# Sharing filler matmuls evenly over attention steps in a fused attention and gated-FFN block on one core

## The chip, the core and the metric

One core of a Trainium2 chip runs the whole program. The core has a matmul engine (TensorE, PE in the profile, with its weight loads shown as PEld), VectorE (DVE), ScalarE (ACT), GpSimd (POOL), and SyncE (SP), which here only issues transfers. Each engine works through its own list of instructions in order; they meet through semaphores. Matmuls write into PSUM, eight banks of 128 x 512 float32 numbers; DVE and ACT move results from there to SBUF.

The metric is the time of one execution on the device in microseconds (us). The kernel before is given by three runs, of which the median counts.

## The reference

A transformer block in which attention and a gated feed-forward part run side by side on the same normalized input. S = 2048 tokens, D = 448, H = 16 heads of 28, window W = 256, F = 1792, all bfloat16:

```python
xn = layernorm(x)                                   # over D, eps 1e-5, no weights
q, k, v = split(xn @ wqkv)                          # 16 heads of 28
scores = q @ k.T * 28 ** -0.5
mask = (0 <= i - j) & (i - j < 256)                 # causal, sliding window
o = softmax(where(mask, scores, -1e9)) @ v
out = x + o @ wo + (gelu(xn @ w_gate) * (xn @ w_up)) @ w_down
```

## The kernel before

The tokens are worked in four blocks of 512 (QB, index `qb`), each of four tiles of 128. A block has these kinds of work:

- **prep** (`stat`, `rstd`, `norm`, driven by the generator `gen_prep`): mean and variance on DVE, the reciprocal root on ACT, the normalized rows on DVE; nine small operations a block, handed out one at a time as `aux`.
- **proj** (`gen_proj`): four transposes of normalized tiles on PE, copied to `xnT` by DVE; four head groups of q and k (`pq`, `pk`, cast to `qT` and `kT`); four tiles of v in pairs (`pv`, cast to `v_sb`). The contraction of 448 is three chunks of 128 and one of 64; `mm3` makes the three, `mm_half` the last, two at a time on the two halves of the array.
- **attention** (`attention`): twelve steps, for each of four head groups three pieces `n` of keys. A step makes QK (`sc`, eight small matmuls, four heads side by side), two exponentials on ACT to `p_sb`, and masks on POOL. PV (`ov`, in `finish`) of a step is issued two steps later (`lag`). After the third piece of a group DVE normalizes: transpose of ov (line 328), copy of the sums (329), reciprocal (331), transpose back (333), product to `oN` (334).
- **gates** (`gated`): seven pairs of the 14 chunks of F: gate (`gt`) and up (`u0`) matmuls, gelu on ACT, product on DVE into `hT`. The up part of chunks listed in `early` has been made ahead, by `gen_up`, into `hT`.
- **down** (`gen_down`): for each token tile 18 matmuls into `po` (four of `wo` with oN, 14 of `wd` with hT), the residual added by DVE, and the output transfer issued by SP.

The source order is the order of every engine's list (`tc.manual_schedule()`). Attention alone doesn't fill PE, so generators of other matmuls are interleaved with it as filler, through the class `Feed`: each `yield` names nanoseconds, and `feed.run(ns)` advances the first generator until that much is spent. In a step before, `feed.run(per_step * 0.6)` stands after the masks and `feed.run(per_step * 0.4)` after the PV. What a call spends over its budget is not carried on.

In block 0 proj(0) is made ahead of attention, and the filler is proj(1) and the early up part of four pairs. In blocks 1 and 2 the filler is down of the block before and proj of the next one. In block 3 it is down(2) and the up part of all seven pairs. After the steps the last two PVs are issued, then `feed.drain()` runs what is left, then come the gates.

PSUM before: tag `s`, two tiles of two banks each, for `sc` and `gt`; tag `m`, four banks, for all else, ov included. A tile of a tag waits until the last reader of the tile whose bank it takes has finished.

At the end, a check of all softmax sums (`okc`, `nok`, `flag`) decides whether `general_path`, a slow exact version, has to run; with these inputs it does not. `n_ok` is loaded into a register of every engine after the last tile of down.

## Time and profile before

| | us |
|---|---|
| median of three runs | 290.64 |
| lowest and highest of the three | 289.18, 291.83 |
| profiled execution, device time | 290.42 |
| profiled execution, span from first to last instruction | 288.7 |

The mean granted clock of TensorE in the profiled execution is 0.925 of full speed. The profile lists instructions by engine, source line and tile name, with starts in us from the beginning of the span. Time of an engine inside a stage is read from a table of stretches: each row has the stretch, its length, and then the busy time of PE, PEld, DVE, ACT and POOL, each with the number of instructions, the granted clock, the share of DMA and its GB/s. Other rows are from the list in order of time (start, duration, engine, line, operation, tile written and tiles read, count, and in brackets the idle time before it with what ended it) and from the chain of work that ended last (start, duration, engine, tile, line).

### The profile page before, as it was taken

The page shows a single profiled execution, that of the slowest core. Times are in us where ns is not written, and L with a number is a line of the kernel's source. Part 1 is how long each engine was busy: PE and PEld are TensorE (multiplying, and loading weights), DVE is VectorE, ACT ScalarE, POOL GpSimd, SP SyncE. Part 2 cuts the span into 40 slices and gives each one's busy share as a digit, 9 for nine tenths or more (in the row PEclk, how much of TensorE's full clock was granted, in tenths as well). Part 3 has the DMA queues.
Part 4 walks back from the last instruction along what each step waited for, and adds up shares of the span by engine and source line. Part 5 has one row for each costly group of instructions (what it writes and reads, how often), then busy time and mean ns, then how long its engine had stood idle before and what let it go on. Part 6 is the DMA issues. An engine that isn't in the chain of part 4 may idle for free.

```text
span 288.7 us, 4252 instructions
## 1 busy us (share of the span) xinstructions
PE 253.2 (88%) x1704; PEld 96.9 (34%) x1725; DVE 154.7 (54%) x296; ACT 135.3 (47%) x156; POOL 75.8 (26%) x104
## 2 busy tenths in 40 slices
PE   8997989599999994799999896699999999479992
PEld 3433322223344331233344332233334322123451
DVE  6587887953432979533321677353431396643510
ACT  3535435833654458423365348713364525756300
POOL 6203323600053435300042334600014233530000
PEclk9999979779999997599999999589999999759998
DMA  6999300000010000000000000000001100000011
GB/s 199 372 263 283 102 2 0 1 2 0 0 33 17 16 3 0 3 0 0 0 18 32 18 0 2 0 0 2 0 0 34 33 0 2 0 0 2 0 34 40
DMA packets 9025, 10.94 MB, mean 38 GB/s; under 512 B 616, under 2 KB 7976, under 8 KB 9000
## 3 DMA queue, kind: packets, MB, share of 16 engines
q1 hardware_dynamic: 8312, 9.69, 11.3%
q10 hardware_dynamic: 688, 0.92, 1.0%
q8 instruction: 15, 0.25, 0.4%
q14 instruction: 10, 0.08, 0.1%
HBM read 8.77 MB, written 1.84 MB: 37 GB/s over the span
## 4 chain that ended last, share of the span: by engine, by line
PE 75%; ACT 11%; DVE 7%; issue 3%; POOL 2%; ACTq 0%; POOLq 0%
PE po L233 15%; PE gt L177 14%; ACT p_sb L349 10%; PE u L177 7%; PE sc L344 5%; PE ue L177 5%; PE gt L182 5%; PE po L229 4%; PE pv L177 4%; PE pk L177 3%; PE pq L177 3%; PE ov L323 3%; PE wps L134 3%; POOL p_sb L355 2%; PE pq L182 2%
## 5 line engine op out<-in xcount | busy, mean ns | idle before, releaser
L349 ACT ACTIVATE p_sb<-sc 128x1024 bf16<-128x1024 f32 (+2 forms) x96 | 87.8, 968 | 66.7 <-PE sc L344 66.6
L355 POOL TENSOR_SCALAR_AFFINE_SELECT p_sb<-p_sb 128x512 bf16<-128x512 bf16 (+1 forms) x92 | 69.8, 781 | 175.9 <-ACT p_sb L349 175.9
L233 PE MATMUL po<-wd,hT 128*128 128x448 bf16 x224 | 48.3, 353 | 0.0
L177 PE MATMUL gt<-xnT,wg 128*128 128x512 bf16 x161 | 46.0, 399 | 1.4 <-issue 1.4
L295 DVE TENSOR_TENSOR hT<-ge,u 128x512 bf16<-128x512 bf16 x34 | 21.8, 684 | 34.2 <-ACT ge L293 34.2
L344 PE MATMUL sc<-qT,kT 32*128 32x128 bf16 (+2 forms) x352 | 24.7, 291 | 15.2 <-ACT p_sb L349 13.8
L293 ACT ACTIVATE ge<-gt 128x1024 bf16<-128x1024 f32 x17 | 17.4, 1024 | 41.9 <-PE gt L177 41.9
L238 DVE TENSOR_TENSOR res<-po,x_sb 128x448 bf16<-128x448 f32 x16 | 10.0, 624 | 44.9 <-PE po L233 44.9
L177 PE MATMUL u<-xnT,wu 128*128 128x512 bf16 x99 | 28.8, 394 | 0.2
L323 PE MATMUL ov<-p_sb,v_sb 128*32 128x128 bf16 (+2 forms) x352 | 22.6, 323 | 6.0 <-POOL p_sb L355 5.8
L233 PEld LDWEIGHTS <-hT 128*128 128x128 bf16 x224 | 20.4, 98 | 20.8 <-issue 3.8
L177 PEld LDWEIGHTS <-wg 128*128 128x128 bf16 x168 | 14.3, 101 | 24.8 <-issue 13.4
L177 PEld LDWEIGHTS <-wu 128*128 128x128 bf16 x168 | 15.3, 101 | 21.0 <-issue 7.2
L344 PEld LDWEIGHTS <-kT 32*128 32x128 bf16 x352 | 8.1, 93 | 33.5 <-issue 33.2
L328 DVE STREAM_TRANSPOSE l<-ov 128x512 f32<-128x512 f32 x16 | 11.4, 710 | 14.9 <-PE ov L323 14.9
L177 PE MATMUL ue<-xnT,wu 128*128 128x512 bf16 x62 | 18.4, 406 | 0.4 <-issue 0.3
L281 ACT ACTIVATE ge<-gt 128x1024 bf16<-128x1024 f32 x11 | 11.3, 1024 | 13.6 <-PE gt L177 13.6
L182 PE MATMUL gt<-xnT,wgu 64*128 64x512 bf16 x45 | 15.1, 398 | 0.0
L229 PE MATMUL po<-wo,oN 128*128 128x448 bf16 x64 | 14.8, 353 | 0.0
L323 PEld LDWEIGHTS <-v_sb 128*32 128x32 bf16 x352 | 7.0, 99 | 22.7 <-issue 19.8
L177 PE MATMUL pq<-xnT,wqp 128*128 128x512 bf16 x45 | 12.9, 381 | 1.8 <-DVE xnT L173 1.6
L282 DVE TENSOR_TENSOR hT<-ge,hT 128x1024 bf16<-128x1024 bf16 x11 | 7.6, 693 | 12.3 <-ACT ge L281 12.3
(67 smaller groups left out, 247.8 us busy)
## 6 DMA issues: line engine op xcount, KB each, us to landing
out_dram<-res SPq DMA_DIRECT2D x16, 112.0 KB, 1.7
wd<-in_B_w_down_dram SPq DMA_DIRECT2D x1, 1568.0 KB, 13.3
wu<-in_B_w_up_dram SPq DMA_DIRECT2D x1, 1344.0 KB
wg<-in_B_w_gate_dram SPq DMA_DIRECT2D x1, 1344.0 KB, 16.3
x_sb<-in_A_x_dram SPq DMA_DIRECT2D x1, 896.0 KB
wraw<-in_A_wqkv_dram ACTq DMA_DIRECT2D x1, 672.0 KB
x_sb<-in_A_x_dram SPq DMA_DIRECT2D x1, 448.0 KB
wo<-in_A_wo_dram SPq DMA_DIRECT2D x4, 98.0 KB
```

The lines of the kernel that those rows point to most:

```text
L177: nc.tensor.matmul(ps, lhsT=lhs(c), rhs=rhs(c), start=start and c == 0, stop=stop and c == 2, skip_group_check=True)
L182: nc.tensor.matmul(ps, lhsT=lhs[p0:p0 + 64], rhs=rhs[p0:p0 + 64], start=start, stop=stop, tile_position=(p0, 0), skip_group_check=True)
L229: nc.tensor.matmul(po[:, 0:D], lhsT=oN[:, g, cs], rhs=wo[:, g, :], start=(g == 0), stop=False, skip_group_check=True)
L233: nc.tensor.matmul(po[:, 0:D], lhsT=hT[:, f, cs], rhs=wd[:, f, :], start=False, stop=(f == NF - 1), skip_group_check=True)
L281: nc.scalar.activation(out=ge[:, :, :], in_=gt[:, :, :], func=ACT.Gelu_apprx_tanh)
L293: nc.scalar.activation(out=ge[:, :, :], in_=gt[:, :, :], func=ACT.Gelu_apprx_tanh)
L295: nc.vector.tensor_tensor(out=hT[:, f + i, :], in0=ge[:, i, :], in1=us[i][:, :], op=ALU.mult)
L323: nc.tensor.matmul(ov[32 * j:32 * j + 32, q0:q0 + nq], lhsT=v_sb[:, kt, h, :], rhs=p_sb[:, j, col:col + nq], start=(n == 0 and i == 0), st ...
L328: nc.vector.transpose(out=l1[:, :, :].rearrange("p a b -> p (a b)"), in_=ov[:, :])
L344: nc.tensor.matmul(ss[j // 2][:, j % 2, col:col + nq], lhsT=kT[r, g, kt * P:(kt + 1) * P], rhs=qT[r, g, qb * QB + q0:qb * QB + q0 + nq], s ...
L349: nc.scalar.activation(out=p_sb[:, 2 * i:2 * i + 2, 0:ncol], in_=ss[i][:, :, 0:ncol], func=ACT.Exp, scale=SCALE)
L355: nc.gpsimd.affine_select(out=reg, in_=reg, pattern=mid + [[1 if diag else -1, P]], compare_op=ALU.is_ge, fill=0.0, base=0 if diag else -1 ...
```

## The change

- `Feed` keeps the nanoseconds that are left (`left`), and `share(parts)` spends `left / parts`; the last part spends all. An attention step has one call, `feed.share(12 - 3 * g - n)`, at its end. The costs that the generators name are adjusted.
- In a step, the PV of two steps before now stands directly ahead of QK. Two aux operations follow each step, where it was one.
- `attention` returns `rest`, which issues the last two PVs of the block. `gated` calls it (`then`) after the first of its seven pairs.
- PSUM: `m` has three banks, and a new tag `o` of one bank holds ov. In the gates every fourth up accumulator (`u0`) takes the bank of `o`, for the first time the second one of the second pair.
- proj is split into `gen_v` and `gen_qk`. For each next block the order is transposes, v, q and k. At the start, v of block 0 is made among the transposes of block 0; then group 0 of q and k; groups 1 to 3 are filler of block 0's attention, ahead of proj(1). A step of a group waits in the source until its group is made (`done`).
- Block 0 has no early up part. Prep of block `qb + 1` is handed out in block `qb`; four of its operations (the statistics) come ahead of attention 0.
- Transfers at the start: v's weights ahead of those of q and k, which move from ACT's queue to SP's; the last rows of v's weights move to ACT's. Warm-up matmuls are fewer and placed otherwise.
- The casts of q in block 0 go from ACT to DVE, those of v in block 0 all to ACT.
- `n_ok` is loaded after two thirds of the last down instead of at its end.

```diff
+    def share(self, parts):
+
+        self.run(max(self.left, 0) / parts if parts > 1 else 1e12)
...
-    nc.scalar.dma_start(out=wraw[:, 0:3, :], in_=rows(A_wqkv, 0, 3)[:, :, 0:2 * D])
+    nc.sync.dma_start(out=wv[:, 0:3, :], in_=rows(A_wqkv, 0, 3)[:, :, 2 * D:3 * D])
+    for p0 in (0, 64):
+        nc.scalar.dma_start(out=wv[p0:p0 + 64, 3, :], in_=A_wqkv[384:448, 2 * D:3 * D])
+    nc.sync.dma_start(out=wraw[:, 0:3, :], in_=rows(A_wqkv, 0, 3)[:, :, 0:2 * D])
...
+    def gen_proj(qb):
+        for t in range(4 * qb, 4 * qb + 4):
+            transp(t, nc.vector.tensor_copy)
+            yield 450
+        yield from gen_v(qb, (4 * qb, 4 * qb + 2))
+        yield from gen_qk(qb, range(4))
+
+    PROJ, QK1 = 4 * 450 + 2 * 1530 + 4 * 1700, 1700
+    DOWN = 4 * 3400
+    UP1 = 1700
...
-    def gated(qb, early):
+    def gated(qb, early, then):
...
         for f in range(0, NF, 2):
+            if f == 2:
+                then()
...
-            us = [psum.tile([P, QB], f32, name="u0", tag="m", bufs=4) for _ in range(2)]
+            us = []
+            for _ in range(2):
+                tag, n = ("m", 3) if nu % 4 < 3 else ("o", 1)
+                us.append(psum.tile([P, QB], f32, name="u0", tag=tag, bufs=n))
+                nu += 1
...
-                o_t[g] = psum.tile([P, QB], f32, name="ov", tag="m", bufs=4)
+                o_t[g] = psum.tile([P, QB], f32, name="ov", tag="o", bufs=1)
...
         for g in range(4):
+            while (qb, g) not in done:
+                feed.run(1)
             for n in range(3):
...
+                if len(pend) >= lag:
+                    finish(*pend.pop(0))
                 ss = [psum.tile([P, 2, QB], f32, name="sc", tag="s") for _ in range(2)]
...
-                feed.run(per_step * 0.6)
                 pend.append((g, n, pc, p_sb))
-                if len(pend) > lag:
-                    finish(*pend.pop(0))
-                next(aux, None)
-                feed.run(per_step * 0.4)
-        while pend:
-            feed.run(per_step)
-            finish(*pend.pop(0))
+                for _ in range(2):
+                    next(aux, None)
+                feed.share(12 - 3 * g - n)
+
+        def rest():
+            while pend:
+                finish(*pend.pop(0))
+        return rest
...
     feed = Feed()
-    feed.add(gen_proj(0))
-    aux = gen_prep(1)
-    while feed.gens:
-        feed.run(900)
-        next(aux, None)
...
+    feed.add(gen_qk(0, range(4)), 4 * QK1)
     for qb in range(NB):
...
         if qb == 0:
-            early = range(0, 8, 2)
-            feed.add(gen_proj(1))
-            feed.add(gen_up(0, early))
-            aux = gen_prep(2)
+            aux = gen_prep(1)
+            feed.run(QK1)
+            for _ in range(4):
+                next(aux, None)
+            feed.add(gen_proj(1), PROJ)
...
-        attention(qb, feed, (1600, 2000, 2000, 2000)[qb], aux, 2)
+        rest = attention(qb, feed, aux, 2)
...
-        feed.drain()
...
-        gated(qb, early)
+        gated(qb, early, rest)
...
+    feed.run(DOWN / 3)
+    n_ok = nc.values_load(flag[0:1, 0:1], min_val=0, max_val=P)
+    feed.share(1)
...
-    n_ok = nc.values_load(flag[0:1, 0:1], min_val=0, max_val=P)
```

## The prediction

> **What bounds the kernel now.** I read the page's busy shares first, then busy time by stage (columns: stretch, its length, busy us of PE, PEld, DVE, ACT, POOL with instruction counts, granted clock; the cuts are each block's first QK and first gate, and the point where block 1's filler runs out), then the same table over stretches of 3.41 us, since every change of the granted clock falls on that grid.

> ```profile
> PE 253.2 (88%) x1704; PEld 96.9 (34%) x1725; DVE 154.7 (54%) x296; ACT 135.3 (47%) x156; POOL 75.8 (26%) x104
> ```
> ```profile
> 0.00:21.58 21.58, 19.67 (x92) 7.77 (x94) 14.05 (x40) 8.57 (x20) 6.07 (x12) 1.00 0.93 278
> 21.58:57.57 35.99, 29.76 (x223) 10.16 (x225) 30.18 (x62) 20.14 (x28) 14.31 (x20) 0.90 0.28 79
> 57.57:76.34 18.77, 18.14 (x85) 6.27 (x83) 8.03 (x15) 7.20 (x8) 0.00 (x0) 0.91 0.00 1
> 76.34:107.77 31.43, 30.40 (x246) 12.78 (x248) 18.80 (x38) 17.14 (x19) 11.10 (x15) 1.00 0.05 16
> 107.77:119.55 11.78, 6.09 (x83) 2.17 (x81) 9.07 (x16) 9.04 (x9) 7.43 (x10) 0.68 0.00 0
> 119.55:144.14 24.59, 23.81 (x115) 8.66 (x115) 10.27 (x18) 7.20 (x8) 0.00 (x0) 0.95 0.00 1
> 212.18:256.28 44.10, 37.97 (x315) 14.11 (x317) 21.45 (x35) 25.79 (x26) 18.46 (x24) 0.91 0.04 11
> 256.28:269.48 13.20, 12.82 (x59) 4.37 (x58) 6.48 (x11) 6.15 (x6) 0.00 (x0) 0.91 0.00 1
> ```
> ```profile
> 23.27:26.68 3.41, 2.20 (x16) 0.99 (x18) 2.64 (x9) 1.10 (x2) 1.69 (x2) 1.00 1.10 236
> 36.92:40.33 3.41, 2.12 (x16) 0.70 (x15) 2.92 (x6) 1.95 (x5) 1.76 (x3) 1.00 0.00 0
> 40.33:43.75 3.42, 3.42 (x17) 0.96 (x16) 2.49 (x6) 0.00 (x0) 0.11 (x1) 0.50 0.02 5
> 94.95:98.36 3.41, 2.85 (x19) 0.95 (x20) 3.27 (x7) 1.16 (x3) 1.52 (x2) 1.00 0.01 2
> ```

> PE bounds the program, with one kind of hole. Block 1's attention runs from 76.34 to 119.55: 31.43 us with filler, PE nearly full, then 11.78 us after the filler has run out, with PE at 6.09 us and the clock at 0.68. Block 3 has the same hole inside its 44.10 us, and block 2 repeats block 1 stage by stage. In it the exponentials set the step:

> ```profile
> 110.71 1.95 ACT p_sb L349 x2
> 113.34 1.95 ACT p_sb L349 x2
> ```

> A step takes 2.63 us there. The third table also shows that a short idle is enough to halve the clock: 1.29 us of idle (3.41 - 2.12) was followed by a stretch at 0.50, while 1.21 us (3.41 - 2.20) was not.

> **The change part by part.** The sum is against the profiled execution, 290.42 us (span 288.7), 0.2 below the median of 290.64. Prices of PE work first, each the distance of two rows: a token tile of down, a q/k head group, a pair of v tiles, a gate pair, a gate pair whose up part is done early.

> ```profile
> 276.65 0.76 PE po L229 x4
> 280.05 0.76 PE po L229 x4
> 15.12 0.75 PE pq L177 x3
> 16.85 0.75 PE pq L177 x3
> 18.57 1.24 PE pv L177 x6
> 20.11 1.24 PE pv L177 x6
> 126.06 0.75 PE gt L177 x3
> 129.29 0.75 PE gt L177 x3
> 260.27 1.40 PE gt L177 x6
> 261.99 1.40 PE gt L177 x6
> ```
> ```profile
> 93.66 1.41 DVE L173 COPY xnT<-tp 128x512 bf16<-128x512 bf16 x4
> 90.58 1.69 PE L233 MATMUL po<-wd,hT 128*128 128x448 bf16 x8
> 92.20 0.40 PE L344 MATMUL sc<-qT,kT 32*128 32x384 bf16 x8
> 92.53 0.55 PE L233 MATMUL po<-wd,hT 128*128 128x448 bf16 x2
> ```

> So 3.40, 1.73, 1.54, 3.23 and 1.72 us; four transposed tiles about 1.5 (their copies take 1.41). A QK costs 0.33 (92.20 to 92.53) and 0.11 to get into it: eight po matmuls from 90.58 at 3.40/18 = 0.19 each end at 92.09. I price a PV like a QK.

> **Even filler, PV next to QK (blocks 1 and 2).** Before, every run call overshot its budget and forgot the overshoot, so 2000 asked became some 3000 a step. The new share divides what is left, so twelve steps get 2.3, 2.6, 2.6, 2.3, 2.6, 2.0, 2.0, 1.9, 2.4, 1.7, 1.7, 1.1 us by the diff's own costs. PE: 4 x 3.40 + 1.5 + 2 x 1.54 + 4 x 1.73 = 25.1, plus ten PV+QK pairs at 0.77 (one way in instead of two) and two QK alone at 0.44, 8.6: 33.7 us against 31.43 + 11.78 = 43.2. A step of 2.8 clears the 2.63 of the exponentials.

> **What is late next.** ov now has one bank of its own. The first PV of group g+1 stands at the head of PE's queue until group g's normalization has left it, and QK, the filler and thereby ACT wait behind. That chain on DVE:

> ```profile
> 37.27 0.73 DVE l L328
> 39.27 0.70 DVE oN L334
> 40.11 0.40 PE ue L182
> L329 DVE COPY l_all<-l x16: 174/268/1035, 38.0 to 257.1; 128x16 f32<-128x16 f32 x16
> ```
> ```profile
> L216 DVE CAST v_sb<-pv x14: 592/614/625, 20.2 to 179.4; 128x448 bf16<-128x448 f32 x14
> 13.47 0.69 DVE L203 CAST kT<-pk 128x512 bf16<-128x512 f32 x1 [2.13 <-PE pk L182]
> 76.31 1.28 ACT L424 ACT_TABLE_LOAD   x1
> 77.60 1.94 ACT L349 ACTIVATE p_sb<-sc 128x1024 bf16<-128x1024 f32 x2
> ```

> PE goes on 2.84 us after the chain starts, up to 0.86 later when L329 takes 1.035 instead of 0.17; I take 3.1. Group 0's chain (step 4, filler 2.6) costs 0.3. Group 1's falls in step 7 among the v tiles: three m banks are left, and the fourth pv needs a cast of 0.61 queued behind the chain, while PE has 0.4 + 0.3 + 0.7 us of work: wait 2.4. Group 2's (step 10) stands behind the last 0.35 us of two casts (0.69 each), and PE has QK and a q/k group, 2.2 us: wait 1.2. At step 1, QK waits for the first exponentials, which start 1.26 after the table load (77.60 against 76.34) and end 3.2 after it, with 2.6 us of PE work: 0.6. Sum 4.5, so 38.2: -5.0 a block. Both ends: nothing, or 6 if L329 is slow each time.

> **Last PV among the gates.** The two PVs move between pair 0 and pair 2, 0.8 us of PE, and the wait for their masks goes. But pair 2's second up accumulator takes the ov bank, so it waits for the chain, and the chain stands on DVE behind pair 0's products:

> ```profile
> 68.75 1.02 ACT L293 ACTIVATE ge<-gt 128x1024 bf16<-128x1024 f32 x1 [1.56 <-PE gt L177]
> 69.80 1.28 DVE L295 TENSOR_TENSOR hT<-ge,u 128x512 bf16<-128x512 bf16 x2 [1.89 <-ACT ge L293]
> ```

> That pair ended on PE at 69.2, its products at 71.08: 1.9 later. With the chain of 2.84 PE may go on 4.7 after pair 0; PVs, two triples and a half pair fill 2.4. Wait 2.3 (1.5 to 3.2), and all gates queue behind it. Gates: 7 x 3.23 + 0.8 + 2.3 + 0.7 (the turn to the next block, as now) = 26.4 against 24.59: +1.8. Blocks 1 and 2: -3.2 each, -6.4.

> **Block 3** has no prep and no v, and its up pairs were early before too: 13.6 + 7 x 1.72 + 8.6 = 34.2, waits 0.6 + 0.3 + 0.95 + 0.95 (an up pair per step beside each chain), 37.0 against 44.10; gates 12.8 against 13.2. -7.5.

> **Start and block 0.** v leads, then only q/k group 0 stands ahead of the first QK.

> ```profile
> 10.99 0.59 ACT L173 COPY xnT<-tp 128x512 bf16<-128x512 bf16 x1 [0.28 <-PE tp L172]
> ```

> The last xnT copy still ends near 11.6: six warm-ups fewer are taken up by two v casts on ACT. Then a v pair's rest, group 0 (1.73), and two DVE casts (1.38) that nothing covers: first QK at 16.0 (15 to 18) against 21.58, -5.6. The moved loads (wv ahead of wraw, one more issue on ACT's queue, the same bytes on SP's) I cost at nothing: the xnT copies cover them; gone, it costs what wraw lands later, about 1. Attention 0: PE 3 x 1.73 + 11.5 + 7.3 = 24 (its pieces are shorter), but DVE had 30.18 busy of 35.99 here; it loses the early up casts and gets q's casts, and four stats now precede group 1's casts. By DVE's order group 1's and 2's casts hold up banks for 1.8 + 0.9 + 0.5, the three chains for 1.2 + 2.0 + 0.9, and in the last steps, which have little filler left, the exponentials for 2.6: 34.0 against 35.99, -2.0. Gates without early ups: 26.4 against 18.77, +7.6. Block 0: 0.0 (-5 to +5).

> Prep a block later, its two operations a step, and the flag's load pulled ahead: nothing, they lie under the filler and under down's last tiles.

> **Sum without the clock:** 0.0 - 6.4 - 7.5 = -13.9: 276.5. The nine chain waits in attention are 14.1 of the waits in it. Before has two chains under filler, with 1.29 and 0.56 idle; at their mean nine cost 8.3. I take the middle, -2.9.

> **The clock.** By the 3.41 us rows a wait over about 1.25 us that falls into one stretch costs a stretch at half clock, 1.7 us of work. The gates' waits (three) and step 7's (two) are long enough in nine of ten positions: 1.7 x 0.9 x 5 = 7.9; block 0's, half under DVE's own backlog, 1.7. Together +9.6: 276.5 - 2.9 + 9.6 = 283.

> [...]

> **The rivals.** (a) The waits are there, the clock stays whole: 283 - 9.6 = 274. For it: 1.21 us idle did nothing; against it: 1.29 did. (b) The chains hide as well as the one at 94.95 (0.56 each, so 5.0 for 14.1), with a whole clock: 276.5 - 9.1 = 267. Against it: both rows are from steps with 3 us of filler. (c) No real change: the waits stand in full and those of step 10 and block 0 halve the clock too, some 7.6 stretches, +13: 289.5. (d) Slower: two whole casts (1.38) stand ahead of the chain at all nine groups: 283 + 9 x 1.38 = 295. It decides from 1.2 us per group on ((293.5 - 283)/9). For it: DVE is 84% busy in block 0; against it: down's steps cast once in 3.4 us. (e) That even filler doesn't reach PE, since ACT's 2.63 sets the step, is (c)'s limit: only the steps with 1.7 or less are there.

> **How the numbers follow.** 1% of 290.64 is 2.9 us, about what a measurement of this kernel can tell from no change: faster is below 287.7, slower above 293.5. Forecast 0.42 (277 to 289, 0.04 of it above 287.7), (a) 0.20, (b) 0.08, (c) 0.17, (d) 0.13. Faster 0.38 + 0.20 + 0.08 = 0.66, same 0.21, slower 0.13. From 267 to 292 leaves out (d) and half of (b), 0.17.

> **What would show it.** Attention 1 and 2 at 38 to 40 us with no stretch of low PE at their end; PE waiting on oN (L334) at the first PV of groups 1 to 3 and once, over 2 us, in pair 2 of the gates of blocks 0 to 2; single stretches of 3.41 us at half clock behind these; the first QK near 16. I am wrong if the time between two blocks' first QK stays near 67.8 or drops below 60, or if the clock stays at 1.00 through gates that have that wait.

## The result, and the profile after

| | before | after |
|---|---|---|
| median, us (four runs of each) | 290.67 | 276.56 |
| lowest and highest, us | 289.18, 291.83 | 276.25, 277.72 |
| profiled execution, device time and span, us | 290.42, 288.7 | 276.25, 274.5 |
| mean granted clock | 0.925 | 0.975 |

The changed kernel takes 0.9525 of the time of before, 95% interval 0.9473 to 0.9576. Times in this document are medians that leave out executions over 1.5% above the fastest of the same kernel, which are two of qk_first and one of one_pool_pv_apart. The first lines are the page's of the changed kernel; then busy time by stage (the start, attention and gates of block 0, of block 1 and of block 3), cut as in the prediction (columns as there).

```profile
span 274.5 us, 4234 instructions
PE 239.5 (87%) x1695; PEld 93.3 (34%) x1714; DVE 150.1 (55%) x294; ACT 133.7 (49%) x154; POOL 75.7 (28%) x104
```
```profile
0.00:16.09 16.09, 12.06 (x57) 4.63 (x60) 9.10 (x28) 7.16 (x17) 6.21 (x12) 1.00 0.91 289
16.09:47.89 31.80, 24.20 (x205) 9.20 (x209) 26.03 (x53) 17.88 (x26) 13.47 (x19) 1.00 0.50 131
47.89:75.89 28.00, 25.41 (x120) 8.95 (x122) 10.18 (x18) 8.92 (x10) 0.63 (x1) 0.94 0.00 1
75.89:114.50 38.61, 34.53 (x308) 14.28 (x309) 25.08 (x51) 24.50 (x27) 17.25 (x22) 0.96 0.04 13
114.50:140.76 26.26, 23.91 (x130) 8.74 (x131) 11.47 (x20) 8.88 (x10) 1.23 (x2) 1.00 0.00 1
205.62:242.46 36.84, 34.27 (x298) 13.17 (x302) 19.79 (x34) 24.12 (x25) 17.25 (x22) 1.00 0.04 14
242.46:255.18 12.72, 12.67 (x71) 4.41 (x72) 7.11 (x13) 7.82 (x8) 1.23 (x2) 1.00 0.01 1
```

Block 2 repeats block 1 (38.61 and 26.25). PE is still the bound, but the hole at the end of each attention is gone: block 1's attention was 43.21 us and is 38.61, block 3's was 44.10 and is 36.84. The start gives 5.5 us. The gates of blocks 0 to 2 got longer. The groups of PE's waits on other engines (us in all, times, longest), and five of these waits in the list in order of time, show what is in the way now:

```profile
PE ov L348 <- DVE oN L359: 8.2, 6, 1.8
PE u L187 <- DVE oN L359: 5.9, 3, 2.1
PE pv L182 <- DVE v_sb L205: 4.4, 2, 2.2
PE pk L182 <- DVE qT L221: 1.9, 2, 1.6
```
```profile
55.74 0.39 PE L187 MATMUL u<-xnT,wgu 64*128 64x512 bf16 x1 [2.13 <-DVE oN L359]
100.94 0.91 PE L182 MATMUL pv<-wv,xnT 128*128 128x448 bf16 x2 [2.18 <-DVE v_sb L205]
112.12 0.40 PE L348 MATMUL ov<-p_sb,v_sb 128*32 128x128 bf16 x8 [1.58 <-DVE oN L359]
122.29 0.39 PE L187 MATMUL u<-xnT,wgu 64*128 64x512 bf16 x1 [1.90 <-DVE oN L359]
240.06 0.40 PE L348 MATMUL ov<-p_sb,v_sb 128*32 128x128 bf16 x8 [0.97 <-DVE oN L359]
```

All are waits for a PSUM bank: the gates' second up accumulator of pair 2 for the ov bank (55.74 and 122.29; pairs go by their first chunk `f`, 0, 2, 4 and so on, so pair 2 is the second); the fourth v tile in step 7 (100.94); the first PV of group 3 (112.12 and, in block 3, 240.06). The step-7 wait is read on DVE, where the normalization of group 1 runs from 97.43 to 100.36 and the first v cast, which PE needs, stands behind it:

```profile
97.43 0.72 DVE L353 STREAM_TRANSPOSE l<-ov 128x512 f32<-128x512 f32 x1 [0.95 <-PE ov L348]
99.67 0.69 DVE L359 TENSOR_TENSOR oN<-ov,rb 128x512 bf16<-128x512 f32 x1
100.28 1.15 DVE L205 CAST v_sb<-pv 128x448 bf16<-128x448 f32 x2
```

The clock is halved in three stretches between the first QK and the end of the gates: behind the wait in block 0's gates (0.50 from 56.24) and behind the two step-7 waits (0.50 from 100.61 and from 165.47). Stretches of 3.41 us on the grid of the clock:

```profile
35.76:39.17 3.41, 2.09 (x16) 0.70 (x12) 3.27 (x7) 1.51 (x2) 2.81 (x4) 1.00 0.00 0
52.83:56.24 3.41, 1.28 (x7) 0.32 (x6) 2.71 (x6) 0.00 (x0) 0.00 (x0) 1.00 0.00 0
56.24:59.65 3.41, 3.41 (x9) 1.18 (x8) 1.19 (x2) 1.02 (x1) 0.00 (x0) 0.50 0.00 0
97.20:100.61 3.41, 1.56 (x21) 0.61 (x14) 3.04 (x6) 2.08 (x3) 2.36 (x4) 1.00 0.03 7
100.61:104.03 3.42, 3.09 (x22) 0.77 (x22) 1.97 (x4) 0.12 (x1) 1.01 (x1) 0.50 0.00 0
121.09:124.51 3.42, 2.22 (x10) 0.99 (x11) 1.11 (x2) 1.02 (x1) 0.00 (x0) 1.00 0.00 0
124.51:127.92 3.41, 3.41 (x19) 1.31 (x17) 1.39 (x3) 1.02 (x1) 0.00 (x0) 1.00 0.00 0
```

PE is idle for 1.32 us in the first of these rows, and the stretch that follows it, 39.17 to 42.59, is at 1.00; by the prediction's bound of 1.25 one should have.

### The profile page after: what moved, and what is told of

Same layout as the page of the kernel before. It is cut to its first block, busy times and chain, and to the rows that moved or that the text cites. A ratio compares the mean times of both kernels' runs of the same rounds, so it can differ in the third digit from the quotient of the medians.

```text
span 274.5 us, 4234 instructions
## 1 busy us (share of the span) xinstructions
PE 239.5 (87%) x1695; PEld 93.3 (34%) x1714; DVE 150.1 (55%) x294; ACT 133.7 (49%) x154; POOL 75.7 (28%) x104
## 3 DMA queue, kind: packets, MB, share of 16 engines
q1 hardware_dynamic: 8552, 10.27, 12.7%
HBM read 8.77 MB, written 1.84 MB: 39 GB/s over the span
## 4 chain that ended last, share of the span: by engine, by line
PE 67%; DVE 19%; ACT 6%; issue 2%; DMA 2%; POOL 1%; SPq 0%; ACTq 0%; DVEq 0%; POOLq 0%
PE po L251 14%; PE gt L182 14%; PE u L182 8%; PE ov L348 4%; PE gt L187 4%; PE sc L373 4%; PE po L247 4%; PE pv L182 3%; ACT p_sb L378 3%; DVE rb L358 3%; DVE oN L359 3%; DVE l L353 3%; PE ue L182 3%; PE pq L182 2%; ACT ge L318 2%
## 5 line engine op out<-in xcount | busy, mean ns | idle before, releaser
L320 DVE TENSOR_TENSOR hT<-ge,u 128x512 bf16<-128x512 bf16 x42 | 27.0, 684 | 47.1 <-ACT ge L318 47.1
L318 ACT ACTIVATE ge<-gt 128x1024 bf16<-128x1024 f32 x21 | 21.5, 1024 | 53.7 <-PE gt L182 53.7
L182 PE MATMUL gt<-xnT,wg 128*128 128x512 bf16 x164 | 45.8, 389 | 1.0 <-ACT p_sb L378 0.8
L182 PE MATMUL u<-xnT,wu 128*128 128x512 bf16 x123 | 34.6, 385 | 0.2
L373 PE MATMUL sc<-qT,kT 32*128 32x128 bf16 (+2 forms) x352 | 22.2, 281 | 4.2 <-ACT p_sb L378 1.7
L348 PE MATMUL ov<-p_sb,v_sb 128*32 128x128 bf16 (+2 forms) x352 | 18.3, 286 | 8.6 <-DVE oN L359 8.2
L182 PEld LDWEIGHTS <-wu 128*128 128x128 bf16 x168 | 15.6, 99 | 20.3 <-issue 4.2
L182 PEld LDWEIGHTS <-wg 128*128 128x128 bf16 x168 | 13.8, 99 | 24.2 <-issue 12.8
L187 PE MATMUL u<-xnT,wgu 64*128 64x512 bf16 x42 | 13.2, 382 | 5.9 <-DVE oN L359 5.9
L221 DVE CAST qT<-pq 128x512 bf16<-128x512 f32 x16 | 11.0, 686 | 13.4 <-PE pk L187 13.4
L158 DVE TENSOR_SCALAR xn<-x_sb,mv_all,rstd_all 128x448 bf16<-128x448 bf16 (+1 forms) x32 | 12.6, 441 | 8.7 <-ACT rstd_all L150 8.6
L182 PE MATMUL pv<-wv,xnT 128*128 128x448 bf16 x48 | 12.0, 379 | 4.8 <-DVE v_sb L205 4.4
L182 PE MATMUL pk<-xnT,wkp 128*128 128x512 bf16 x46 | 12.9, 379 | 2.0 <-DVE qT L221 1.9
```

Source lines behind the costliest of these rows:

```text
L158: nc.vector.tensor_scalar(out=xf[:, lo:lo + n], in0=x_sb[:, t, src:src + n], scalar1=mv_all[:, t, 0:1], scalar2=rstd_all[:, t:t + 1], op0= ...
L182: nc.tensor.matmul(ps, lhsT=lhs(c), rhs=rhs(c), start=start and c == 0, stop=stop and c == 2, skip_group_check=True)
L187: nc.tensor.matmul(ps, lhsT=lhs[p0:p0 + 64], rhs=rhs[p0:p0 + 64], start=start, stop=stop, tile_position=(p0, 0), skip_group_check=True)
L318: nc.scalar.activation(out=ge[:, :, :], in_=gt[:, :, :], func=ACT.Gelu_apprx_tanh)
L320: nc.vector.tensor_tensor(out=hT[:, f + i, :], in0=ge[:, i, :], in1=us[i][:, :], op=ALU.mult)
L348: nc.tensor.matmul(ov[32 * j:32 * j + 32, q0:q0 + nq], lhsT=v_sb[:, kt, h, :], rhs=p_sb[:, j, col:col + nq], start=(n == 0 and i == 0), st ...
```

## The experiments

Each timed kernel ran beside the kernel before on the same chip: 290.26 us in the first two groups of runs, 289.64 in the third. Line numbers in the experiments' kernels can differ by a few from those above.

### First group: is the gain the even filler, and does the ov bank take some of it back?

**share_undone**: the changed kernel with the old budgets; what is left over is run ahead of the gates.

```diff
-                feed.share(12 - 3 * g - n)
+                feed.run(per_step * 0.6)
+                feed.run(per_step * 0.4)
...
-        rest = attention(qb, feed, aux, 2)
+        rest = attention(qb, feed, (1600, 2000, 2000, 2000)[qb], aux, 2)
...
+        feed.run(1e12)
         for _ in aux:
             pass
         if qb not in hTs:
```

> The changed kernel with only the sharing undone: a step calls for 0.6 and 0.4 of 2000 ns (1600 in block 0) as before, overshoot forgotten, and what is left runs ahead of the gates. If the even filler is what closed the holes, they come back: blocks 1 to 3 get some 3 us of filler in each of the first eight steps and then four steps of about 2.6 us with PE near half busy and a half clock, 2.5 to 4 us more per block, 285 us (281 to 290). If the gain came from the start, the early q/k group and the PVs among the gates, it stays at 277 to 279.

Measured: 307.4 us, 1.0608 of before (1.0546 to 1.0669): slower than before, and 30.8 more than the changed kernel. The hole is back (first row below: the end of block 1's attention), and there is a second one ahead of it, in which PE stands for a whole stretch of 3.41 us with half clock behind it (0.50 from 98.37 to 101.79):

```profile
110.00:124.20 14.20, 7.53 (x79) 2.55 (x78) 7.59 (x15) 8.46 (x10) 6.30 (x8) 0.81 0.00 0
94.96:98.37 3.41, 0.05 (x1) 0.05 (x1) 3.38 (x6) 0.90 (x1) 1.72 (x2) 1.00 0.00 0
```
```profile
PE tp L177 <- DVE res L256: 7.1, 2, 3.6
```

By the profile a transpose there waits for a bank that `res` has to leave, and on DVE `res` stands behind a chain and the norms of the prep, which the change moved into this block. Front-loaded filler reaches the transposes while the norms are still being made. So the other parts of the change lean on the even filler; undoing it in the changed kernel costs more than it was worth by itself. The direction was expected, the size was not.

**share_alone**: the kernel before with `share` in place of the two `run` calls, and nothing else of the change.

```diff
-                feed.run(per_step * 0.6)
...
-                feed.run(per_step * 0.4)
+                feed.share(12 - 3 * g - n)
...
-                feed.add(gen_proj(qb + 1))
+                feed.add(gen_proj(qb + 1), 10220)
```

> The kernel before with only the sharing added (left divided by the steps left, once a step), all else as it was: four m banks with ov among them, PV behind QK, v last, early up part in block 0, the last two PVs ahead of the gates. If the sharing carries the gain, each of blocks 1 to 3 loses its hole of 11.8 us but pays two PVs that wait for the last masks: about 3 us less per block, 281 us (277 to 285). If waits of PV and casts on the chain take it all back, 288 to 291.

Measured: 269.73 us, 0.9283 of before (0.9247 to 0.9319). One part of the change alone gains 20.5 us, more than all of it together (14.1). Block 1's attention takes 39.54 us with the clock whole:

```profile
75.13:114.67 39.54, 34.75 (x326) 14.29 (x326) 25.21 (x53) 26.18 (x28) 18.41 (x24) 1.00 0.04 13
```

So the other parts, put on top of it, cost some 7 us net, and one or more of them must be a loss.

**u_late**: the changed kernel, with the gates taking the ov bank first in pair 4 (the third) in place of pair 2.

```diff
-                tag, n = ("m", 3) if nu % 4 < 3 else ("o", 1)
+                tag, n = ("o", 1) if nu % 4 == 1 and nu > 1 else ("m", 3)
```

> The changed kernel, but in the gates the up accumulators use the ov bank for the first time in the third pair instead of the second. If PE's waits of 2.13, 1.90 and 1.90 us in pair 2 of blocks 0 to 2 are for the bank, they go, and in block 0 the stretch at half clock (1.7 us) behind them: 276.6 - 5.9 - 1.7 = 269 us (268 to 271). If the chain on DVE behind pair 0's products is itself what is late, the wait turns up at the next m bank and it stays at 275 to 277.

Measured: 267.67 us, 0.9256 (0.9195 to 0.9317), 8.9 less than the changed kernel, where 7.6 was expected. The gates of blocks 0 to 2 fall from 28.00, 26.26 and 26.25 to 23.80, 23.98 and 23.98 (this row is block 1's):

```profile
111.41:135.39 23.98, 23.63 (x133) 8.65 (x131) 11.48 (x20) 8.88 (x10) 1.23 (x2) 1.00 0.00 1
```

That is 8.7 us, the sum of the three waits (5.9), one half-clock stretch (1.7), and 0.4 around each wait. The wait for the ov bank in the gates is a pure loss, and a choice of bank removes it.

**ov_copy**: ACT copies ov to SBUF as soon as the third PV is done, and the chain works from the copy.

```diff
             if n == 2:
+                ovs = work.tile([P, QB], f32, name="ovs", bufs=2)
+                nc.scalar.copy(out=ovs[:, :], in_=ov[:, :])
+                ov = ovs
```

> The changed kernel, but ACT copies ov (float32) to SBUF after a group's last PV, and the normalization works from the copy, so that the bank is free after some 0.8 us instead of 2.8. If the price of the change is the time that the bank is held, PE's waits on oN go (8.2 us at the first PV of a group in six places, 5.9 us in the gates) and half of the half-clock stretches; the waits of v and q/k casts behind the chain stay; ACT has 16 copies of 0.6 us more in its idle time: 266 us (262 to 270). If DVE's chain as such is late, the waits move to the m banks: 270 to 276.

Measured: 269.85 us, 0.9316 (0.9274 to 0.9358), 6.7 less than the changed kernel and at the upper end of what was expected. No wait of PE for oN is left and the gates are as short as in u_late, but PE now waits longer for its other banks:

```profile
PE pv L182 <- DVE v_sb L205: 5.9, 2, 2.9
PE pk L182 <- DVE qT L221: 4.4, 4, 1.6
```

They were 4.4 and 1.9. By this reading a bank that comes free early helps less where the chain still holds up the casts behind it on DVE, and three m banks don't reach over it.

### Second group: the division of the banks, the order of the filler, the clock

**one_pool**: ov and all of the gates' up accumulators from the common pool of four m banks again (`bufs=4` in every tile of that tag); everything else as changed.

```diff
-            wps = psum.tile([P, QB], f32, name="wps", tag="m", bufs=3)
+            wps = psum.tile([P, QB], f32, name="wps", tag="m", bufs=4)
...
-                tag, n = ("m", 3) if nu % 4 < 3 else ("o", 1)
-                us.append(psum.tile([P, QB], f32, name="u0", tag=tag, bufs=n))
+                us.append(psum.tile([P, QB], f32, name="u0", tag="m", bufs=4))
...
-                o_t[g] = psum.tile([P, QB], f32, name="ov", tag="o", bufs=1)
+                o_t[g] = psum.tile([P, QB], f32, name="ov", tag="m", bufs=4)
```

> The changed kernel with ov and all of the gates' up accumulators taken from the common pool of four m banks again (as before the change), everything else as changed. Theory 'the own ov bank is what takes back part of the gain': waits of PE for oN at the first PV (8.2 us in all) fall to some 2 to 3, the waits in the gates' pair 2 (5.9) and their half-clock stretches go: gates of blocks 0 to 2 about 23.3, attention 1 and 2 about 38.3, 266 to 269. Rival 'the wait is for the chain on DVE, whichever bank it holds': filler waits for it instead (m banks), attention stays at 39, the gates wait all the same: 273 to 277.

Measured: **260.05 us, 0.8954 of before (0.8910 to 0.8998)**, the fastest of all, 16.5 less than the changed kernel and better than expected. PE's waits for DVE, and the stages of block 1:

```profile
PE pv L182 <- DVE oN L357: 3.3, 2, 1.7
PE pq L182 <- DVE oN L357: 2.7, 3, 1.2
PE ov L346 <- DVE oN L357: 1.2, 1, 1.2
PE pk L182 <- DVE qT L221: 1.1, 1, 1.1
```
```profile
70.02:106.09 36.07, 33.33 (x308) 14.24 (x310) 25.07 (x51) 25.38 (x28) 17.62 (x23) 1.00 0.04 14
106.09:130.07 23.98, 23.52 (x130) 8.65 (x131) 11.47 (x20) 7.99 (x9) 0.85 (x2) 1.00 0.00 1
```

The four groups of waits of the changed kernel come to 8.2 + 5.9 + 4.4 + 1.9 = 20.4 us, these four to 8.3. With one half-clock stretch between the first QK and the end of the gates where there were three, that is 12.1 + 2 x 1.7 = 15.5 of the 15.9 between the two spans (274.5 and 258.6). The rival, that the wait comes from the chain whichever bank it holds, falls for its larger part: with one bank the first PV of the next group and the gates have to wait for the chain, with four they take another one. Some 7 us of waits for oN stay, now for the most part at the filler's banks. Against share_alone (269.73) one_pool is 9.7 us faster, so without the division of the banks the other parts together are a gain.

**qk_first**: in the filler, q and k ahead of v again.

```diff
-        yield from gen_v(qb, (4 * qb, 4 * qb + 2))
         yield from gen_qk(qb, range(4))
+        yield from gen_v(qb, (4 * qb, 4 * qb + 2))
```

> The changed kernel with the filler's q/k head groups ahead of the v tiles again for blocks 1 to 3 (block 0 keeps v first). Theory: the step-7 wait of 2.2 us (a fourth v tile without a bank while group 1's chain holds DVE) goes from there with its half-clock stretch, but the v tiles now come in the last steps, where they meet group 2's chain; the same wait stands there: attention 1 and 2 stay within 0.7 us of 38.6 (first QK to first PE work of the gates), total 276.6 +- 2. Rival 'v ahead costs, since casts of 0.61 from two tiles come faster than those of a q/k group': waits on v_sb (4.4) and half-clock stretches in attention go, 2 x (1.5 + 1.7) less: 270.

Measured: 279.78 us (279.44, 279.78 and 281.92), 0.9625 (0.9602 to 0.9648), 3.2 more than the changed kernel. The profiled execution is that of 281.92, so its stages show more than the median does. Attention 1 and 2 (39.09 and 37.69) are within 1 us of the changed kernel's (0.7 was expected), the waits on v_sb are gone and those for oN at the first PV are 11.6 in place of 8.2: there the wait moved, as the theory had it. What neither had is a new wait in block 0, with a half-clock stretch behind it (0.50 from 31.06 to 34.47):

```profile
27.64:31.06 3.42, 0.80 (x8) 0.42 (x7) 2.97 (x6) 1.24 (x2) 2.77 (x4) 1.00 1.04 344
```
```profile
PE pq L182 <- DVE xnT L178: 3.9, 3, 2.6
```

A q/k group reads all four transposed tiles at once, so it waits for the last copy of `xnT`; a pair of v tiles reads only its own two. Block 0's attention and gates take 34.73 and 29.54 in place of 31.80 and 28.00. From the first QK to the end of the gates five stretches are at half clock where there were three, 3.4 of the 5.7 us between the two spans (280.2 and 274.5). So v ahead was worth its place, by a small margin and for a reason that the prediction didn't give.

**zero_full** and **zero_row** fill part of the gates' wait in pair 2 with matmuls that add zeros to a gate accumulator: five that use the whole array, or eight that use 32 of its rows. The expectations speak of block 0; the edit acts on pair 2 of blocks 0, 1 and 2.

```diff
             half(gt[:, 1, :], f + 1, True, 0, ts, True, False)
+            if f == 2:
+                for _ in range(5):
+                    nc.tensor.matmul(gt[:, 0, :], lhsT=warm[:, 0:P], rhs=warm[:, :], start=False, stop=True, skip_group_check=True)
             half(us[1][:, :], f + 1, False, 1, ts, True, False)
```

> The changed kernel with five matmuls more of 128 rows x 128 columns x 512 that add zeros to a gate accumulator, in block 0's gate pair 2, ahead of the place where PE waits 2.13 us for the ov bank (block 0 alone). They take 5 x 0.21 = 1.07 us of that wait. Theory 'share of the array' (a 3.41 us stretch is followed by half clock where its matmuls, weighted by rows x columns of the array in use, fill under some 0.38 of it): the stretch that held 0.20 now holds 0.51, so the half-clock stretch behind that wait goes, 1.7 us less, 274.9. Rival 'idle time' (over 1.25 us idle in a stretch): idle falls to 1.1, so it goes here too. Third possibility, the clock falls for another reason than this wait: stays at 276.6 with the half-clock stretch in place.

> The changed kernel with eight zero matmuls at the same place that use only 32 rows x 128 columns of the array each, 8 x 0.21 = 1.7 us of the 2.13 us wait. Theory 'share of the array': they weigh a quarter, 0.20 + 0.125 = 0.33, still under 0.37, so the half-clock stretch in gates 0 stays: 276.6 (up to 0.3 more). Rival 'idle time': PE is idle for 0.4 us only, so the half-clock stretch goes: 274.9. The two runs are told apart by the granted clock behind the wait, more than by the time.

Measured: 276.09 (0.9514, 0.9491 to 0.9538) and 276.16 us (0.9520, 0.9493 to 0.9547), both within 0.5 of the changed kernel. Neither has a half-clock stretch behind the wait in block 0's gates: three matmuls of a gate or up accumulator take 0.81 or 0.82 us there, where the changed kernel has 1.31 to 1.48. In zero_full that agrees with both theories. In zero_row it proves nothing, since the grid of the clock lay otherwise against the program: by the author's reading a stretch ended within the filled wait (53.2 to 55.4), and neither half of it was long enough for either theory. In zero_full, by the same reading, a half-clock stretch came up in attention 0 instead; the mean clock is 0.978 with 0.975 in the changed kernel. The pair left the question open.

### Third group: two placements, and the clock again

**one_pool_pv_first** and **one_pool_pv_apart**, both on one_pool: the last two PVs ahead of the gates, and a step's PV in the middle of its filler instead of ahead of its QK.

```diff
-            if f == 2:
+            if f == 0:
                 then()
```
```diff
-                if len(pend) >= lag:
-                    finish(*pend.pop(0))
                 ss = [psum.tile([P, 2, QB], f32, name="sc", tag="s") for _ in range(2)]
...
-                feed.share(12 - 3 * g - n)
+                feed.share(24 - 6 * g - 2 * n)
+                if len(pend) > lag:
+                    finish(*pend.pop(0))
+                feed.share(23 - 6 * g - 2 * n)
```

> one_pool (260.05) with the last two PVs of each block ahead of its gates instead of between gate pairs 0 and 1. Theory 'placing them among the gates hides the last mask': in one_pool the last q/k matmuls of block 1's attention end at 106.1 and the last mask on POOL at 106.95, so PE would wait 0.85 us in each of four blocks, and gates start later: 263.5. Rival 'worth nothing' (share_alone, which has them ahead of the gates, spends on blocks 1 and 2 what u_late spends): 260.

> one_pool (260.05) with a step's PV after the first half of the step's filler, not ahead of its QK. Theory 'one way in instead of two' (0.11 us of PE for each, 36 to 40 pairs): 4 us more, 264. Rival 'worth nothing or less, since QK then comes 0.33 us earlier and with it the exponentials, and a PV half a step later meets its mask surely finished': 258 to 261.

Measured: 265.09 us (0.9127, 0.9070 to 0.9183) and 268.3 (0.9244, 0.9189 to 0.9298), so 5.0 and 8.3 more than one_pool. In the first the last PVs wait for their masks,

```profile
PE ov L346 <- POOL p_sb L382: 3.2, 7, 1.1
```

which was 0.2 in one_pool, and there is one more half-clock stretch (1.7): 4.7 of the 5.0. Among the gates the PVs are covered. The second costs twice the 4 us that the extra ways into a group of small matmuls were priced at. Where the rest of it comes from was not settled. On the common pool, both placements of the change are gains.

**rows32** and **full32** repeat the question on the clock with 32 zero matmuls, long enough to fill whole stretches wherever the grid lies (again in pair 2 of blocks 0 to 2).

```diff
+                for _ in range(32):
+                    nc.tensor.matmul(gt[:, 0, :], lhsT=warm[0:32, 0:P], rhs=warm[0:32, :], start=False, stop=True,
+                                     tile_position=(0, 0), skip_group_check=True)
```

> The changed kernel with 32 zero matmuls that use 32 rows x 128 columns of the array, at the ov wait in block 0's gate pair 2: 6.8 us in which PE is never idle and at least one whole 3.41 us stretch is filled with matmuls that weigh a quarter. Theory 'share of the array': the stretch after the first whole one runs at half clock (0.50) though PE was not idle; with the slower matmuls some 276.5 + 4.7 + 1.7 to 5 = 283 to 287. Rival 'idle time': no half clock there, 276.5 + 4.7 = 281, less 1.7 for the one half-clock stretch that stood behind the wait: 279.5.

> The control to rows32: the same 32 zero matmuls with 128 rows x 128 columns. Both theories: no half clock in block 0's gates, 276.5 + 4.7 - 1.7 = 279.5. A half clock there too would throw out both.

Measured, one run each: 310.16 and 293.67 us; the forecasts of the times were for one block's zeros, not three. Stretches of rows32, then of full32:

```profile
55.19:58.60 3.41, 3.41 (x18) 1.35 (x18) 2.47 (x6) 0.00 (x0) 0.00 (x0) 1.00 0.00 0
58.60:62.01 3.41, 3.41 (x10) 1.17 (x8) 0.00 (x0) 0.00 (x0) 0.00 (x0) 0.50 0.00 0
133.70:137.11 3.41, 3.41 (x17) 1.49 (x16) 0.62 (x1) 0.00 (x0) 0.00 (x0) 1.00 0.00 0
137.11:140.53 3.42, 3.42 (x10) 1.14 (x8) 0.00 (x0) 0.00 (x0) 0.00 (x0) 0.50 0.00 0
```
```profile
56.84:60.25 3.41, 3.41 (x18) 1.55 (x16) 0.00 (x0) 0.00 (x0) 0.00 (x0) 1.00 0.00 0
60.25:63.66 3.41, 3.41 (x17) 1.34 (x16) 0.00 (x0) 0.94 (x1) 0.00 (x0) 1.00 0.02 5
```

With matmuls on a quarter of the rows PE has no idle time at all in 133.70 to 137.11, and the next stretch is at 0.50. With the same matmuls on all rows PE has none in 56.84 to 60.25 either, and the next stretch is at 1.00. "Idle time" falls as what alone decides. The theory "share of the array" agrees with both runs, at a quarter of the rows and at all of them; where between the two the clock would change, they don't show.

## Why the prediction was right, and where it was off

The forecast was 283, a gain of 7.6 us, and the gain was 14.1, nearly twice that. 276.56 lies in the range of 267 to 292, but just under the forecast's own band of 277 to 289. The direction, the main gain and the places of the waits were right; the clock term was too large, and the other terms were on the high side by some 2 us.

- **Even filler** was the main gain, as forecast. Attention 1 and 2 were to take 38.2 without the clock. They took 38.61 with one half-clock stretch of 1.7 us, so 36.9: PE's work was 34.53 - 1.7 = 32.8 where 33.7 was summed, and its waits 4.1 where 4.5 were. Block 3 came at 36.84 and 12.72, forecast 37.0 and 12.8.
- **The start**: 16.09 against 16.0. Of the moved transfers one wait of PE shows, 0.43 us for v's weights.
- **Block 0**: attention 31.80 against 34.0. PE's work was as summed (24.20 against 24); its waits were 7.6, priced at 9.9. Gates 28.00, of which 1.7 is the clock: 26.3 against 26.4.
- **Gates of blocks 1 and 2**: 26.26 and 26.25 against 26.4, with a wait of 1.90 in pair 2 (5.9 for all three), forecast 2.3. **Step 7**: 2.18 against 2.4. **Step 10**: 1.58 against 1.2. **Block 3's** last chain wait: 0.97 against 0.95.
- **The middle between two readings of the chain waits** took 2.9 off the stages. It rests on a miscount: the terms that add up to 14.1 are twelve, three in each block, and not nine. At the mean of 1.29 and 0.56 twelve cost 11.1, so the middle is 12.6, which takes off 1.5 and gives a forecast of 284.4. Measured they cost 12.6 (8.2 at the first PVs, 4.4 at the fourth v tiles). Without the clock the stages came out 5.2 below the forecast ones, of which the chain waits are 1.5. PE's work in attention 1 and 2 is 1.8, and the other waits of attention 0, for casts and exponentials, are 1.3. So the idea of the middle was right, and that the miscount brought the forecast 1.4 nearer to the result is luck.
- **The clock** is the term that was mis-sized: +9.6 was forecast, three stretches at 1.7 = 5.1 came. The step that failed is "By the 3.41 us rows a wait over about 1.25 us that falls into one stretch costs a stretch at half clock": the term was counted from idle time. The bound rested on two stretches of before, 1.29 us idle with 0.50 behind it (36.92) and 1.21 with 1.00 (23.27). In the changed kernel, up to the end of the gates, 1.60, 1.32 and 1.29 us of idle time (the stretches at 18.69, 35.76 and 28.93) have 1.00 behind them, and only 2.13, 1.85 and 1.84 (52.83, 97.20 and 162.05) have 0.50. rows32 has 0.50 behind a stretch without any. So these runs show no bound on idle time alone. That the share of the array in use decides was the author's theory; the limits for it in the expectations, near 0.38, were estimates that no run measured.

  The gates' waits of blocks 1 and 2 lay across a boundary of the grid. The one that ended at 122.29 lay in two stretches with 0.74 and 1.20 us of idle time (117.68 and 121.09), the one that ended at 187.16 in two with 0.74 and 1.21 (182.53 and 185.95), all under the prediction's own 1.25; its "nine of ten positions" was an estimate. So one of the prediction's own signs of being wrong came true in two blocks: the clock stayed at 1.00 through the gates of blocks 1 and 2, which had the wait, 1.90 us each.

  The profiled execution (276.25) lies 6.75 under the forecast: 4.5 from here, and 2.3 from the point above (5.2 less the 2.9 taken off).
- **The rivals**: (a), a whole clock, 274, came nearer than the forecast (2.6 us against 6.4), but a whole clock is not what happened: three half-clock stretches came, and without them the same waits would have given some 271. (b) did not hold: the chain waits cost 12.6 and not 5.0. (c), (d) and (e) fell: every stage came out at the forecast (within 0.1) or under it, but for the half-clock stretch in block 0's gates and in attention 1 and 2.
- **What the prediction didn't ask**: it took the ov bank of its own as given, priced its waits well, and didn't price the alternative. The change as it stands is 16.5 us of waits and clock short of the same change with one pool, and 6.8 short of the even filler alone.

## What to carry to other kernels

When a change bundles several parts, price what each would do without the others: here one part of it gained 20.5 us by itself, and undoing a division of PSUM banks that looked like housekeeping gave 16.5 more. Here the bank kept for one use made its next users wait 14.1 us in all (8.2 and 5.9) for the chain behind the last one; in the shared pool, where they take any bank that is free, the waits for that chain came to 7.2. So divide a pool only when the trace shows that the shared one is what waits. And spread filler by what is left, not by a fixed budget that is overshot and forgotten.

## What was not expected of the hardware

```profile
18.69:22.11 3.42, 1.82 (x10) 0.59 (x8) 2.78 (x7) 1.90 (x4) 2.63 (x4) 1.00 1.03 248
22.11:25.52 3.41, 3.10 (x36) 1.17 (x36) 3.41 (x9) 1.11 (x3) 0.75 (x2) 1.00 1.06 294
```

In the kernel before, 1.29 us of idle time (36.92) had 0.50 behind it. Whether filler of whole-array matmuls keeps the clock up in an attention stage by its shape, apart from the time that it fills, was not shown.
